# The mish MLP's first product by Strassen's seven block products

## The chip, the cores and the metric

One core of a Trainium2 chip. The metric is the device time of one execution in microseconds, the median of several runs; the profile is that of one execution.

## The reference

Three parts follow one another on 2304 tokens (4 batches of 576): a landmark attention, a gated product, and the mish MLP that the change is in. Weights are given in float64, everything is computed as float32.

```python
x = landmark_attention(q, k, v)            # [2304, 512]
y = ((x @ w1) * (x @ w2) @ w3) @ w_out     # the gated product, [2304, 512]
h = y @ w_in                               # [2304, 2048]
g = h * np.tanh(np.log1p(np.exp(np.minimum(h, 20.0))))   # mish
out = g @ w_out2                           # [2304, 512]
```

## The kernel before, in words

Float32 products are made from float32r matmuls: each operand is split into a high part (a copy, on ACT) and a low part (a difference, on DVE or POOL), and `mm3` (L194 to L197) issues three matmuls, high x high, high x low and low x high. A weight block of 128 x 512 float64 is loaded into a raw buffer as pairs of 32-bit words and decoded to float32 by four steps: `top_bits` (`da`, L207 on ACT or L209 on DVE), `sign` (`dm`, L213, DVE), `rescale` (`ds`, L216, ACT) and `join` (`db`, L220, DVE).

Up to the end of the gated product the order of the work is written out by hand. `step` names a piece of work, `ORDER` (L27) is a long string of these names, and `issue` (L284) emits them one after another; within an engine the instructions run in that order. The steps that the change touches: `m`, `xa`, `xb`, `xc`, `xm` make the gate's halves `h`; `sh u k` and `sl u k` (L913) split `h` for half-batch `u` (288 tokens, eight of them) into one of two buffers; `y u m` (L920) multiplies it by the folded weights, 4 x 24 matmuls of 288 columns for a half-batch, and `ye` evicts the result to `Y`. The last `y` steps, 3 0 to 7 3, run with nothing but splits beside them on TensorE's side: I call them the y stage. `ld x`, `da x`, `dm x`, `ds x`, `db x`, `hi x`, `lo x` bring in and split 32 blocks of the mish weights (`w_in` and `w_out` in turns of four); 26 of them are decoded and 20 split inside `ORDER`, and `yh`, `yl` split the first tile of `Y`.

Then comes the mish stage, emitted by the loop at L1140. Tokens go in tiles of 512 (four and one of 256), `d_ff` in 16 chunks of 128; one pair of tile and chunk is a tick. `p2` (L1117) issues for tick n:

```python
z_mm(n)       # 4 mm3: 12 matmuls into one of banks 0 to 3
o_mm(n - 2)   # one mm3 for each 128 tokens into banks 4 to 7
tick(n)       # ACT: mish twice (L1113, L1114); DVE: their difference (L1115)
```

Beside the first tile's ticks it splits the last 12 weight blocks and decodes the last 6 (loads on SP's queue, as everywhere); at the end of a tile it splits the next tile's `Y` and evicts the output. All split weights then stay in SBUF, in buffers of earlier stages (`wpart`, L949). `swap` (L902) closes the attention's pool and opens the buffers `hs`.

Of the kernel before, what the change touches and what calls it, by code (L numbers as in the profile page):

```python
# [154 lines left out]
def kernel(  # L155
# [883 lines left out]
    for k in range(4):  # L1039
        add_ys(k)  # L1040
# [141 lines left out]
```

## Time and profile before

| | us |
|---|---|
| median of 3 runs | 767.44 |
| lowest and highest | 767.3, 768.48 |
| span of the profiled execution | 765.2 |

The page gives the profiled execution's span, from its first instruction to its last, and no other time for it. In the profile PE is TensorE's matmuls, PEld its weight loads, DVE, ACT and POOL the vector, scalar and GpSimd engines, SP the engine that issues the loads. Durations of matmuls overlap, so the distance between starts says what one costs. "L1113" is a line of the kernel; an operand such as `ps<-hs,W` names the tile written and the tiles read, without buffer numbers, and late tiles have the names `ys`, `wx`, `gx` and the like.

### The profile page before, as it was taken

How to read it: one execution, taken by the hardware profiler on the slowest of the kernel's cores; microseconds unless marked ns; L12 is line 12 of the kernel's file. 1: busy time of each engine (PE TensorE's matmuls, PEld its weight loads, DVE VectorE, ACT ScalarE, POOL GpSimd, SP SyncE). 2: the span in 40 equal slices, each digit the busy share in tenths (PEclk: the TensorE clock that was granted, in tenths of full speed). 3: DMA queues.
4: the chain of work that ended last, by engine and by line, in shares of the span. 5: the costliest groups of instructions: out<-in, count | busy, mean ns of one | idle time of the engine just before them, and what ended most of it. 6: DMA issues, size and time to landing. Idle time of an engine off the chain costs nothing.

```text
span 765.2 us, 12842 instructions
## 1 busy us (share of the span) xinstructions
...
## 2 busy tenths in 40 slices
...
PEclk9999999999999999999999999999999999999999
...
GB/s 329 372 284 69 153 132 250 152 81 142 57 165 139 84 111 52 196 128 122 56 110 0 1 1 55 1 1 0 56 0 1 1 0 56 1 0 1 56 1 28
DMA packets 37243, 65.90 MB, mean 86 GB/s; under 512 B 2624, under 2 KB 19392, under 8 KB 37184
## 3 DMA queue, kind: packets, MB, share of 16 engines
q1 hardware_dynamic: 37040, 64.96, 25.0%
...
## 4 chain that ended last, share of the span: by engine, by line
PE 89%; DMA 6%; DVE 2%; ACT 1%; SPq 0%; issue 0%; ACTq 0%
PE ps L195 27%; PE ps L197 26%; PE ps L196 26%; PE ps L360 4%; DMA raw<-in_w3T_dram 3%; DMA raw<-in_wo_dram 2%; PE ps L851 2%; PE ps L650 1%; PE ps L454 1%; DMA raw<-in_w_dram 1%; DVE raw L213 1%; PE ps L532 1%; PE ps L591 1%; PE ps L510 0%; PE ps L570 0%; ACT raw L207 0%
## 5 line engine op out<-in xcount | busy, mean ns | idle before, releaser
L1113 ACT ACTIVATE emx<-ps 128x512 f32<-128x512 f32 (+1 forms) x80 | 44.3, 554 | 131.5 <-PE ps L197 131.5
L1115 DVE TENSOR_TENSOR gx<-emx,gx 128x512 fp32r<-128x512 f32 (+1 forms) x40 | 25.6, 639 | 155.1 <-ACT gx L1114 155.1
L195 PE MATMUL ps<-hs,W 128*128 128x288 f32 (+2 forms) x304 | 92.9, 306 | 0.0
L196 PE MATMUL ps<-hs,W 128*128 128x288 f32 (+2 forms) x304 | 92.3, 304 | 0.0
L197 PE MATMUL ps<-hs,W 128*128 128x288 f32 (+2 forms) x304 | 92.2, 303 | 0.0
L1115 DVE TENSOR_TENSOR hs<-emx,hs 128x512 fp32r<-128x512 f32 (+1 forms) x40 | 25.5, 639 | 136.6 <-ACT hs L1114 136.6
L213 DVE TENSOR_SCALAR raw<-raw 128x512 uint16<-128x512 uint16 x84 | 67.2, 840 | 29.2 <-ACT raw L207 28.7
L195 PE MATMUL ps<-AT,M 128*128 128x288 f32 x256 | 79.1, 309 | 1.7 <-ACT a L224 1.4
L196 PE MATMUL ps<-AT,M 128*128 128x288 f32 x256 | 75.5, 295 | 0.0
L197 PE MATMUL ps<-AT,M 128*128 128x288 f32 x256 | 75.5, 295 | 0.0
L360 PE MATMUL ps<-wo,raw 128*128 128x512 f32 x128 | 63.2, 617 | 7.2 <-DVE raw L220 5.4
L207 ACT ACTIVATE raw<-raw 128x512 int32<-128x512 uint16 x64 | 43.2, 679 | 50.4 <-DMA raw<-in_w3T_dram 14.6
L216 ACT ACTIVATE raw<-raw 128x512 f32<-128x512 f32 x84 | 55.5, 675 | 19.5 <-DVE raw L213 19.4
L195 PEld LDWEIGHTS ps<-hs,W 128*128 128x128 f32 x304 | 57.0, 188 | 3.0 <-issue 0.4
L196 PEld LDWEIGHTS ps<-hs,W 128*128 128x128 f32 x304 | 57.4, 189 | 1.4
L197 PEld LDWEIGHTS ps<-hs,W 128*128 128x128 f32 x304 | 57.4, 189 | 1.3
L195 PEld LDWEIGHTS ps<-AT,M 128*128 128x128 f32 x256 | 48.0, 188 | 11.8 <-issue 3.7
L196 PEld LDWEIGHTS ps<-AT,M 128*128 128x128 f32 x256 | 48.1, 188 | 0.0
L197 PEld LDWEIGHTS ps<-AT,M 128*128 128x128 f32 x256 | 48.1, 188 | 0.0
L1114 ACT ACTIVATE gx<-ps 128x512 fp32r<-128x512 f32 (+1 forms) x40 | 22.2, 556 | 61.2 <-PE ps L196 61.2
L360 PEld LDWEIGHTS ps<-wo,raw 128*128 128x128 f32 x128 | 22.6, 196 | 28.8 <-issue 15.1
L1114 ACT ACTIVATE hs<-ps 128x512 fp32r<-128x512 f32 (+1 forms) x40 | 22.2, 556 | 54.7 <-PE ps L196 54.7
...
## 6 DMA issues: line engine op xcount, KB each, us to landing
...
raw<-in_wo_dram SPq DMA_DIRECT2D x22, 512.0 KB, 5.3
raw<-in_w3T_dram SPq DMA_DIRECT2D x16, 512.0 KB, 5.3
raw<-in_wi_dram SPq DMA_DIRECT2D x14, 512.0 KB, 4.0
...
```

Of the source, the lines that this page charges most:

```text
L195: T.matmul(out=o, lhsT=lh, rhs=rh, start=first, stop=False)
L196: T.matmul(out=o, lhsT=lh, rhs=rl, start=False, stop=False)
L197: T.matmul(out=o, lhsT=ll, rhs=rh, start=False, stop=last)
L207: S.activation(w[..., 0], q[..., 1], ACTF.Copy, scale=2.0 ** -13, bias=2.0 ** -14 - 0.5)
L213: V.tensor_scalar(q[..., 1], q[..., 3], 0x8000, None, op0=ALU.bitwise_and)
L216: S.activation(f32(w[..., 1]), f32(w[..., 1]), ACTF.Copy, scale=2.0 ** -112)
L360: T.matmul(out=got(f"acc{i}"), lhsT=f32(got(f"w3{n}")[:, o:o + 128, 0]), rhs=WO0[j // 4][:, j % 4], start=j == 0, stop=j == 7)
L454: T.matmul(out=sc[0:w, i, p * 64:p * 64 + 64], lhsT=st["q"][:, p, t0:t0 + w], rhs=bdk[:, p, :], start=True, stop=True)
L851: T.matmul(out=got(f"p{c}{key}")[32 * i:32 * i + 32, 0:256], lhsT=LT[r, b, 2 * c + par, :], rhs=w12(f"w{bp}{s}{c}")[r, par * 256:par * 256 ...
L1113: S.activation(x, zt[n], ACTF.Mish)
L1114: S.activation(gb(n, 0), zt.pop(n), ACTF.Mish)
L1115: V.tensor_tensor(gb(n, 1), x, f32(gb(n, 0)), op=ALU.subtract)
```

## The change

With `Y` and `w_in` cut into blocks (the contraction of 512 in halves; the tokens in halves; 256 of the 2048 features in halves), the four blocks of z come from seven products of block sums in place of eight products. Token tiles become 768, in halves of 384 (`QT`), three of them; a quarter `q` is 256 features, eight of them; a group `g` is one tile and one quarter, 24 in all. In a group:

- `z_mm(g, p, x, first)` is product P0 to P6: 2 `mm3`, 6 matmuls of 384 columns, into bank 0 or 1, cleared before or added to what is there (P2 is added to P0, P3 and P5 to P1, P6 to P4).
- The rest of the recombination is on DVE: `q_`, `r_` and the blocks `c_of(1)` (two halves of 384) and `c_of(0)`, sums of a bank and an earlier sum; ACT copies P0 out to `s_`. Mish is applied to a bank (384), to `c_of(1)` (768) and to `c_of(0)` (384), twice each as before.
- `o_part(g - 1, i)` issues the output product of the group before in four parts of 9 matmuls of 512, into banks 2 to 7. Group 0 has none.
- `more(i)` emits the work of `WITH[g]` (only in the first tile, groups 0 to 7; six lists to a group, divided by `|`).

The weights of a quarter are summed on POOL (`zs0` to `zs3`), each of the seven sums is split by ACT (`zh`) and DVE (`zl`), 256 columns each, and the quarter is stored in DRAM by `zd` (1.8 MB). A block of the output weights is split by `wh` (ACT) and `wl` (POOL) and stored by `ws` (0.5 MB). This happens for quarters 0 and 1 and blocks 0 and 1 inside `ORDER`, for the others in the first tile's groups, with 20 of the 32 decodes. From group 6 on the weights of a group two ahead are loaded from DRAM (`after_z`, and the loop at the end of a group) into slots that the group just read. Seven operands of a tile's `Y` are formed by `yt` (POOL), `yh` (ACT) and `yl` (DVE): inside `ORDER` for the first tile, in `after_z` of groups 7 and 15 for the others. All transfers are on SP's queue, apart from one at the very end.

In `ORDER` the steps `ld x` to `lo x`, and the old `yh` and `yl`, go; in their places stand `ld n` to `db n` of 12 blocks, two `wh`, `wl` and `ws`, the sums and splits of quarters 0 and 1 and the operands of the first tile. The other steps keep their order.

```diff
-EARLY, RAW6 = 20, 6
...
+WITH = (
+    "zs0 2,zs1 2,zs2 2,wh 2,wl 2,da 16|zh0 2,zl0 2,dm 16,ld 18,ws 2|zh1 2,zl1 2,ds 16,wh 3,wl 3,ld 19,ws 3,da 17|zh2 2,zl2 2,db 16,dm 17|zh3 2,zl3 2,zs3 2,ds 17,db 17,da 18,dm 18|zh4 2,zl4 2,zh5 2,zl5 2,zh6 2,zl6 2,zd 2",
+    "zs0 3,zs1 3,zs2 3,ds 18,db 18,ld 12,ld 13|zh0 3,zl0 3,da 19,dm 19|zh1 3,zl1 3,ds 19,db 19,ld 14,ld 15|zh2 3,zl2 3,da 12,dm 12|zh3 3,zl3 3,zs3 3,ds 12,db 12|zh4 3,zl4 3,zh5 3,zl5 3,zh6 3,zl6 3,zd 3,da 13,dm 13,zs0 4,zs1 4,zs2 4",
+    "ds 13,db 13,wh 4,wl 4|zh0 4,zl0 4,da 14,dm 14,ld 24,ws 4|zh1 4,zl1 4,ds 14,db 14,wh 5,wl 5|zh2 4,zl2 4,da 15,dm 15,ld 25,ws 5|zh3 4,zl3 4,zs3 4,ds 15,db 15,da 24,dm 24|zh4 4,zl4 4,zh5 4,zl5 4,zh6 4,zl6 4,zd 4",
+    "zs0 5,zs1 5,zs2 5,ds 24,db 24,wh 6,wl 6,ld 20|zh0 5,zl0 5,da 25,dm 25,ld 26,ws 6|zh1 5,zl1 5,ds 25,db 25,wh 7,wl 7,ld 21|zh2 5,zl2 5,da 26,dm 26,ld 27,ws 7|zh3 5,zl3 5,zs3 5,ds 26,db 26,ld 22,da 27,dm 27|zh4 5,zl4 5,zh5 5,zl5 5,zh6 5,zl6 5,zd 5,ds 27,db 27,ld 23",
+    "zs0 6,zs1 6,zs2 6,da 20,dm 20|zh0 6,zl0 6,ds 20,db 20,wh 8,wl 8|zh1 6,zl1 6,da 21,dm 21,ld 28,ws 8|zh2 6,zl2 6,ds 21,db 21,wh 9,wl 9|zh3 6,zl3 6,zs3 6,da 22,dm 22,ld 29,ws 9|zh4 6,zl4 6,zh5 6,zl5 6,zh6 6,zl6 6,zd 6,ds 22,db 22",
+    "zs0 7,zs1 7,zs2 7,wh 10,wl 10,da 23,dm 23|zh0 7,zl0 7,ds 23,db 23,ld 30,ws 10|zh1 7,zl1 7,da 28,dm 28|zh2 7,zl2 7,ds 28,db 28|zh3 7,zl3 7,zs3 7,wh 11,wl 11|zh4 7,zl4 7,zh5 7,zl5 7,zh6 7,zl6 7,zd 7,ld 31,ws 11",
+    "wh 12,wl 12,da 29,dm 29|ds 29,db 29,ws 12|da 30,dm 30|wh 13,wl 13,ds 30,db 30|da 31,dm 31,ws 13|ds 31,db 31",
+    "wh 14,wl 14||wh 15,wl 15,ws 14||ws 15|",
+MADE = (0, 1, 2, 3, 8, 9, 10, 11, 4, 5, 6, 7, 16, 17, 18, 19, 12, 13, 14, 15, 24, 25, 26, 27, 20, 21, 22, 23, 28, 29, 30, 31)
...
-    TT = 512
+    QT, TT = S_LEN * B // 6, S_LEN * B // 3
...
-    RAW2 = [kept(f"M{i}", [128, 512, 2], I32, f"raw{i}") for i in range(3)]
-    M = {}
+    RAW2 = kept("M", [128, 3, 512, 2], I32, "raw2")
+    M = []
...
-        HS.extend(pw.tile([128, 8 * 2 * HALF], F32R, name=f"hs{i}") for i in range(2))
-        HS.append(pw.tile([128, 4, 1024], F32R, name="wx"))
-        HS.append(pw.tile([128, 2, TT], F32R, name="gx"))
-        HS.append(pw.tile([128, TT], F32, name="emx"))
+        LATE["pw"] = pw
+        HS.extend(pw.tile([128, 8 * 2 * HALF], F32R, tag=f"hs{i}", name=f"hs{i}") for i in range(2))
+        HS.append(pw.tile([128, 7 * 512], F32R, name="zw0"))
+        HS.append(pw.tile([128, 4, 512], F32, name="wf0"))
...
+    def y_op(p, hl):
+        n, i = {0: (("W0", 0), ("W0", 1)), 2: (("W1", 0), ("W1", 1)), 4: (("H1", 0), ("H1", 1)),
+                3: (("H1", 2), ("H2", 0)), 1: (("H2", 1), ("H2", 2)), 5: (("H3", 0), ("H3", 1)),
+                6: (("M", 0), ("H3", 2))}[p][hl]
+        x = at_m() if n == "M" else late(n, 2048 if n[0] == "W" else 2304, f"y{n}")
+        return x[:, i * 768:(i + 1) * 768].rearrange("p (c s) -> p c s", c=2)
...
+    def wo_slot(u):
+        i = u % 7
+        if i == 0:
+            return at_m()[:, 768:1792]
+        if i == 1:
+            return hs_a()[:, 3584:4608]
+        if i < 4:
+            return late("Y0", 2048, "wy")[:, (i - 2) * 1024:(i - 1) * 1024]
+        return at_m()[:, 1792:2816] if i == 4 else w3_flat(i - 5)[:, 3072:4096]
+
+    def zw_slot(g, p):
+        return (hs_a() if g % 2 else HS[2])[:, p * 512:(p + 1) * 512]
...
+        ops = [(f"ld {n}", "SP", lambda e: x_load(n)), (f"da {n}", "ACT", lambda e: top_bits(e, r())),
+               (f"dm {n}", "DVE", lambda e: sign(r())), (f"ds {n}", "ACT", lambda e: rescale(r()))]
+        if k == 0:
+            return ops + [(f"db {n}", "DVE", lambda e: join(r(), wf(j)[:, i]))]
+        return ops + [
+            (f"db {n}", "DVE", lambda e: join(r())),
+            (f"wh {f}", "ACT", lambda e: copy(e, wo_slot(f)[:, 0:512], f32(r()[..., 0]))),
+            (f"wl {f}", "POOL", lambda e: less(e, wo_slot(f)[:, 512:1024], f32(r()[..., 0]), wo_slot(f)[:, 0:512])),
+            (f"ws {f}", "SP", lambda e: nc.sync.dma_start(out=wod[f], in_=f32(wo_slot(f))))]
...
+        a11, a12, a21, a22 = (0, 0), (0, 1), (1, 0), (1, 1)
+        return [(f"zs0 {q}", "POOL", f(0, a21, a22, ALU.add)),
+                (f"zs1 {q}", "POOL", f(1, 0, a11, ALU.subtract)),
+                (f"zs2 {q}", "POOL", f(a21, a11, a21, ALU.subtract)),
+                (f"zs3 {q}", "POOL", f(1, a12, 1, ALU.subtract))]
...
+    def zp_ops(q, p):
+        return [(f"zh{p} {q}", "ACT", lambda e: copy(e, zw(q, p, 0), z_src(q, p))),
+                (f"zl{p} {q}", "DVE", lambda e: less(e, zw(q, p, 1), z_src(q, p), zw(q, p, 0)))]
+
+    def z_store(q):
+        def f(e):
+            x = (hs_a() if q % 2 else HS[2])[:, 0:3584]
+            nc.sync.dma_start(out=zd[q], in_=f32(x))
+        return (f"zd {q}", "SP", f)
...
+        return [(f"yt4 {t}", "POOL", sub_(y_cuts(t, 0, 1), t_(0), b_(0, 1), b_(0, 0))),
+                (f"yt1 {t}", "POOL", sub_(y_cuts(t, 1), t_(1), b_(1, 1), t_(0))),
+                (f"yt3 {t}", "POOL", sub_(y_cuts(t, 1), b_(0, 1), b_(1, 1), b_(0, 1))),
+                (f"yt5 {t}", "POOL", sub_(y_cuts(t, 0), t_(1), b_(1, 0), t_(1)))]
...
-    def z_mm(n):
-        t, f = divmod(n, NFC)
-        c = slice((f % 4) * 128, (f % 4 + 1) * 128)
-        p = zt[n] = bank[n % 4][:, 0:tiles[t][1]]
-        for k in range(4):
-            u = 8 * (f // 4) + k
...
-    def tick(n):
-        x = E[:, 0:tiles[n // NFC][1]]
-        S.activation(x, zt[n], ACTF.Mish)
-        S.activation(gb(n, 0), zt.pop(n), ACTF.Mish)
-        V.tensor_tensor(gb(n, 1), x, f32(gb(n, 0)), op=ALU.subtract)
...
+    z_bank = bank[0:2]
+    o_bank = bank[2:8]
+    ZT = late("A", 3 * QT, "zt", F32)
+    s_, q_, r_ = (ZT[:, i * QT:(i + 1) * QT] for i in range(3))
...
+    def z_mm(g, p, x, first):
+        for c in range(2):
+            mm3(z_bank[x][:, 0:QT], zw(g, p, 0)[:, c], zw(g, p, 1)[:, c], y_op(p, 0)[:, c], y_op(p, 1)[:, c],
+                first and c == 0, c == 1 and p in (2, 5, 6), True)
+
...
+    def o_part(g, part):
+        if g < 0:
+            return
+        t, q = divmod(g, NQ)
+        if q < NQ - 1:
+            e, i0 = ((0, 0), (1, 0), (1, 3), (0, 3))[part]
+            for i in range(i0, i0 + 3):
+                o_mm(g, e, i)
+            return
+        for i in ((0, 1), (2,), (3, 4), (5,))[part]:
+            for e in range(2):
+                o_mm(g, e, i)
+            o_out(t, i)
+
+    def mish(src_, e, o):
+        S.activation(e, src_, ACTF.Mish)
+        S.activation(o, src_, ACTF.Mish)
...
+    NG = 3 * NQ
+    for g in range(NG):
+        t, q = divmod(g, NQ)
+        todo = WITH[g].split("|") if g < NQ else [""] * 6
+        if q == 5 and t < 2:
+            run(ysum_ops(t + 1)[:3])
+
+        def more(i):
+            for name in filter(None, todo[i].split(",")):
+                name, _, at_e = name.partition("@")
+                e, fn = ops.pop(name)
+                fn(at_e or e)
+
+        def after_z(p):
+            if g + 2 < NG and g + 2 >= NQ:
+                nc.sync.dma_start(out=f32(zw_slot(g + 2, p)), in_=zd[(g + 2) % NQ][:, p * 512:(p + 1) * 512])
+            if q == NQ - 1 and t < 2:
+                run(yp_ops(t + 1, p))
+                if p == 1:
+                    run(ysum_ops(t + 1)[3:])
+
+        z_mm(g, 0, 0, True)
+        S.activation(s_, z_bank[0][:, 0:QT], ACTF.Copy)
+        after_z(0)
+        z_mm(g, 1, 1, True)
+        V.tensor_tensor(q_, z_bank[1][:, 0:QT], s_, op=ALU.add)
+        after_z(1)
+        more(0)
+        o_part(g - 1, 0)
+        more(1)
+        z_mm(g, 2, 0, False)
+        mish(z_bank[0][:, 0:QT], e_of(0), g_of(g, 0, 0)[:, 0:QT])
+        after_z(2)
+        z_mm(g, 3, 1, False)
+        V.tensor_tensor(r_, z_bank[1][:, 0:QT], s_, op=ALU.add)
+        less("DVE", g_of(g, 0, 1)[:, 0:QT], e_of(0), g_of(g, 0, 0)[:, 0:QT])
+        after_z(3)
+        more(2)
+        o_part(g - 1, 1)
+        more(3)
+        z_mm(g, 4, 0, True)
+        after_z(4)
+        z_mm(g, 5, 1, False)
+        after_z(5)
+        V.tensor_tensor(c_of(1)[:, QT:2 * QT], z_bank[0][:, 0:QT], r_, op=ALU.add)
+        V.tensor_tensor(c_of(1)[:, 0:QT], z_bank[1][:, 0:QT], s_, op=ALU.add)
+        mish(c_of(1), e_of(2), g_of(g, 1, 0))
+        more(4)
+        o_part(g - 1, 2)
+        z_mm(g, 6, 0, False)
+        after_z(6)
+        V.tensor_tensor(c_of(0), z_bank[0][:, 0:QT], q_, op=ALU.add)
+        less("DVE", g_of(g, 1, 1), e_of(2), g_of(g, 1, 0))
+        mish(c_of(0), e_of(1), g_of(g, 0, 0)[:, QT:TT])
+        less("DVE", g_of(g, 0, 1)[:, QT:TT], e_of(1), g_of(g, 0, 0)[:, QT:TT])
+        o_part(g - 1, 3)
+        if g:
+            for u in (2 * g - 2 + 7, 2 * g - 1 + 7):
+                if 16 <= u < 2 * NG:
+                    nc.sync.dma_start(out=f32(wo_slot(u)), in_=wod[u % 16])
+        more(5)
```

## Rows read from the trace of the kernel before

**Rows 1.** The page's first line.

```profile
span 765.2 us, 12842 instructions
```

**Rows 2.** Busy time by engine in one stretch; then clock, DMA share, GB/s.

```profile
640.00:680.00 40.00, 40.00 (x178) 33.12 (x177) 6.21 (x10) 9.45 (x17) 0.00 (x0) 1.00 0.00 0
```

**Rows 3.** Timeline of TensorE: start, duration, line, tile, shape.

```profile
366.84 0.30 PE L196 MATMUL ps<-hs,W 128*128 128x288 f32 x1
...
367.89 0.39 PE L195 MATMUL ps<-hs,wx 128*128 128x512 f32 x1
...
600.00 0.39 PE L196 MATMUL ps<-W,hs 128*128 128x512 f32 x1
...
611.79 0.39 PE L197 MATMUL ps<-W,hs 128*128 128x512 f32 x1
...
752.81 0.28 PE L195 MATMUL ps<-hs,W 128*128 128x256 f32 x1
...
754.13 0.28 PE L197 MATMUL ps<-hs,W 128*128 128x256 f32 x1
...
760.95 0.39 PE L197 MATMUL ps<-hs 128*128 128x512 f32 x1
```

**Rows 4.** Groups of ACT by form: count, busy us, mean ns.

```profile
L216 ACT ACTIVATE raw<-raw 128x512 f32<-128x512 f32 x84 | 55.5, 675 | 19.5 <-DVE raw L213 19.4
...
L1114 ACT ACTIVATE gx<-ps 128x512 fp32r<-128x512 f32 x32 | 19.1, 598 | 55.0 <-PE ps L196 55.0
...
L224 ACT ACTIVATE hs<-y 128x512 fp32r<-128x512 f32 x4 | 2.4, 624 | 0.0
...
L224 ACT ACTIVATE hs<-y 128x256 fp32r<-128x256 f32 x4 | 1.6, 409 | 0.0
```

**Rows 5.** Timeline of ACT at the start of the mish stage.

```profile
368.52 1.28 ACT L1113 ACT_TABLE_LOAD   x1
370.81 0.60 ACT L1113 ACTIVATE emx<-ps 128x512 f32<-128x512 f32 x1 [1.01 <-PE ps L197]
371.31 0.59 ACT L1114 ACTIVATE gx<-ps 128x512 fp32r<-128x512 f32 x1
```

**Rows 6.** Groups of DVE by form.

```profile
L889 DVE TENSOR_TENSOR h<-a,ps 128x288 f32<-128x288 f32 x64 | 28.5, 453 | 17.2 <-PE ps L197 13.7 <-ACT M L224 2.0 <-ACT a L224 1.0
...
L229 DVE TENSOR_TENSOR hs<-y,hs 128x512 fp32r<-128x512 f32 x4 | 2.7, 702 | 0.2 <-ACT hs L224 0.2
...
L229 DVE TENSOR_TENSOR hs<-y,hs 128x256 fp32r<-128x256 f32 x4 | 1.7, 419 | 0.0
```

**Rows 7.** Groups of POOL by form.

```profile
L229 POOL TENSOR_TENSOR hs<-raw,hs 128x512 fp32r<-128x512 f32 x2 | 2.6, 1302 | 7.8 <-ACT hs L224 7.8
```

**Rows 8.** The page's DMA queues and DMA issues.

```profile
q1 hardware_dynamic: 37040, 64.96, 25.0%
...
raw<-in_wi_dram SPq DMA_DIRECT2D x14, 512.0 KB, 4.0
```

**Rows 9.** Timelines of DVE and POOL, around 225 us and 380 us.

```profile
225.17 0.88 DVE L229 TENSOR_TENSOR hs<-h,hs 128x288 fp32r<-128x288 f32 x1
...
229.53 0.45 DVE L229 TENSOR_TENSOR hs<-h,hs 128x288 fp32r<-128x288 f32 x1
...
224.93 0.80 POOL L229 TENSOR_TENSOR hs<-h,hs 128x288 fp32r<-128x288 f32 x1
...
356.70 0.77 DVE L213 TENSOR_SCALAR raw<-raw 128x512 uint16<-128x512 uint16 x1 [0.72 <-ACT raw L207]
...
380.77 1.58 DVE L213 TENSOR_SCALAR raw<-raw 128x512 uint16<-128x512 uint16 x1
...
379.98 1.76 POOL L229 TENSOR_TENSOR W<-raw,W 128x512 fp32r<-128x512 f32 x1 [3.40 <-ACT W L224]
```

**Rows 10.** TensorE's waits (total, times, longest us); the page's clock in 40 slices.

```profile
PE ps L360 <- DVE raw L220: 5.4, 3, 3.2
...
PEclk9999999999999999999999999999999999999999
```

More of the change, by code (lines that the diff above doesn't have):

```diff
@@ new lines, in cut, with y_at @@
+    def cut(t, h):
+        a, out_ = t * TT + h * QT, []
+        end = a + QT
+        while a < end:
+            b, s = divmod(a, S_LEN)
+            n = min(end - a, S_LEN - s)
+            out_.append((a - t * TT - h * QT, n, b, s))
+            a += n
+        return out_
+    def y_at(t, k, h, lo, n):
+        for o, m, b, s in cut(t, h):
+            if o <= lo and lo + n <= o + m:
+                return Y[b][:, 2 * k:2 * k + 2, s + lo - o:s + lo - o + n]
+        raise AssertionError
@@ new lines, in y_parts, with yp_ops, hi, lo @@
+    def y_parts(t, p):
+        if p in (1, 4, 5):
+            return [(slice(0, QT), lambda: y_sum(0 if p == 4 else 1))]
+        k, h = {0: (0, 0), 2: (1, 0), 3: (0, 1), 6: (1, 1)}[p]
+        return [(slice(a, z), lambda a=a, z=z: y_at(t, k, h, a, z - a)) for a, z in y_cuts(t, h)]
+    def yp_ops(t, p):
+        def hi(e):
+            for s, x in y_parts(t, p):
+                copy(e, y_op(p, 0)[:, :, s], x())
+        def lo(e):
+            for s, x in y_parts(t, p):
+                less(e, y_op(p, 1)[:, :, s], x(), y_op(p, 0)[:, :, s])
+        return [(f"yh{p} {t}", "ACT", hi), (f"yl{p} {t}", "DVE", lo)]
```

295 lines of the change are left out of this document (167 added, 128 removed), and 233 rows, old and new, of the table ORDER.

## The prediction

> **What bounds the kernel now.** I read the page first, then stretches of the last stage, then single instructions. The execution in the profile spans 765.2 us [rows 1]; the median of the runs is 767.44, so I take 2.24 us as lying around the span and leave it unchanged. In the mish stage TensorE is busy in all of a 40 us stretch while ACT and DVE are busy about a quarter and a sixth of it, and the clock is full [rows 2]. So the stage lasts as long as its matmuls, and their price is the step from one start to the next, not the printed duration, which overlaps: for 512 columns 0.2267 us (600.00 to 611.79 is 52 steps), for 256 0.120 (752.81 to 754.13, 11), for 288 0.131 (366.84 to 367.89, 8) [rows 3]. From 288 to 512 that is 0.427 ns a column, so 384 columns should step by 0.131 + 96 x 0.000427 = **0.172 us**; 0.170 and 0.175 are the ends that the rounding of the rows allows. The stage runs from 367.89 to 760.95 plus one step, 761.18: 393.3 us [rows 3]. Counted from the code: z takes 64 ticks x 12 matmuls of 512 and 16 x 12 of 256, 768 x 0.2267 + 192 x 0.120 = 197.1 us; the output product 864 of 512, 195.9. The sum, 393.0, leaves no gap.
>
> **What the change takes off TensorE.** z becomes 3 tiles x 8 quarters = 24 groups of 7 products of 6 matmuls of 384 columns: 1008 x 0.172 = 173.4 us. The output product keeps its 864. TensorE's own work falls by 197.1 - 173.4 = **23.7 us** (20.7 to 25.7 for the ends of the step). A group is now 7.2 us of z and 8.2 of output, 15.4. The y stage just before keeps TensorE's steps and loses work beside them: from `y 3 0` on 17 decodes and 11 splits go, 3 decodes, 14 splits of 256 and 7 of 768 come (20 of the 32 decodes now fall into the first tile of the mish stage, where 6 did). Its five half-batches of 12.6 us (96 x 0.131) cover that, since the splits that one waits for stand a half-batch early: nothing, and 1 us if the cover is thin.
>
> **What it adds elsewhere.** Before, z needed no adds and had four banks. Now it has two, and the same bank is read, then added to, then cleared, so each product waits for an ACT or DVE read. Prices: an ACT pair of Mish on 384 columns 0.49 us each (0.60 for 512 less 128 columns at the slope of the copies), the second starting before the first ends as at 512 (0.50 after it, of 0.60) [rows 4, 5]; a copy from SBUF 0.41 for 256 and 0.62 for 512, so 0.84 for 768; a decode's ACT step 0.68 [rows 4]. On DVE an add of 384 is 0.56, a split of 256 0.42, a split of 768 0.98, a decode step 0.77 [rows 6, 9]. ACT starts about 0.2 us after the last matmul of a product (12 steps after 367.89 is 370.61, Mish at 370.81) [rows 3, 5]. On POOL a split of 512 is 1.30 [rows 7]; a sum of 256 I take as 0.8, a little over half of that. A loaded block of 512 KB lands in 4.0 us; queue 1 moved 64.96 MB in a quarter of the span, so 340 GB/s when it moves [rows 8].
>
> In **tiles 1 and 2** a group's load is some 4 us on ACT and 5 on DVE, of 15.4. The tightest loop is P5 to the next P0: DVE takes the two halves, 0.75 us after P5; Mish on 768 twice, to 2.4; P6 and its add to 3.9; TensorE comes back to that bank at 2.04 + 1.03 + 2.04 = 5.1. No wait. Reloading weights is 2.9 MB a group, 8.5 us at 340 GB/s, ordered a group and more ahead: nothing, and the whole of it shows only if a load lands 15 us late.
>
> **Group 0** has no output product to fill the waits. Count from P0's start (a product is 1.03 us). ACT: copy of P0 to 1.7, then `wh 2`, `da 16`, `zh0 2`, which stand ahead of Mish, to 3.2, the table load of 1.28 [rows 5] to 4.4, Mish twice to 5.3. P4 clears that bank; TensorE was free at 4.1: 1.25 us. P4, P5 to 7.4. P6 adds to P4's bank after DVE has read it; ahead on DVE are `zl1 2`, `zl2 2` (for which ACT first does `zh1`, `ds 16`, `wh 3`, `da 17`, `zh2`, to 7.65), `db 16`, `dm 17`; the read ends at 9.75: 2.4 us. P6 to 10.8. The next P0 needs DVE's last add, and ahead of that are `zl3 2`, `db 17` and `dm 18`, behind ACT's Mish on 768 (10.3 to 11.9), `zh3 2`, `ds 17`, `da 18`; it ends at 14.5: 3.7 us. Together **7.3**. With none of those extras in the way the same chain gives 1.0, and with each decode step on DVE stretched as below, 10.
>
> **Groups 1 to 6.** 9 output matmuls (2.04 us) now stand between the products, and by the same count a group without a late load waits 0.1 to 0.5: the chain Mish on 768, `zh3`, `ds`, `da`, `dm`, last add is 5.0 us against TensorE's 5.1. Two groups are worse, for what is queued behind what on SP: the store of a quarter's weight sums (`zd`, 1.8 MB, 5.4 us) waits for the last split and stands ahead of loads. In group 1 `ld 12` goes behind `zd 2`, lands about 9 us into the group, and ACT reaches `da 12` 2 us before; the delay passes through `dm 12` and Mish on 768: 2.0 us. In group 3 `ld 26` waits for `wl 6` on POOL and goes behind `zd 4` and `ld 20`: 2.3 us. No row shows such a store; if it held up nothing, both would cost 0.3. The other four take 1.2 together.
>
> POOL works 6.5 us in each of these groups (4 sums, 2 splits), and beside POOL DVE slows: a split of 288 took 0.88 against 0.45 alone, a decode step 1.58 against 0.77, and POOL's own 1.30 became 1.76 [rows 7, 9]. I charge 0.3 us in five groups, 1.5; the ends are 0 and 3 a group (rival below). The Trainium skill (SBUF — State Buffer, "SBUF: two separate sides") says that this is a lock: a GpSimd instruction and a DVE one with two SBUF inputs hold the shared ports in turn, whole instructions at a time. The rows agree with that; taken for every DVE split it gives the second rival's time and not mine.
>
> **Groups 7 and 15** make the next tile's seven operands, a copy and a split of 768 behind each product, and those for P5 and P6 stand ahead of the adds: after P5 a copy to 1.0, a split to 2.0, the read of P4's bank at 2.5, 0.5 us past TensorE's return; then P6's copy (behind Mish) and split, the last add at 6.8 where TensorE is back at 5.6: 1.2. 1.7 each, **3.4** (0 to 5). The tail is the same 4 us: last matmul, a half-bank copy, a store.
>
> Sum: 767.44 - 23.7 + 7.3 + 2.0 + 2.3 + 1.2 + 1.5 + 3.4 = **761.4 us**.
>
> **Rivals.** *The covers hold*: engines run ahead more than I count, so that group 0 costs 5 and the transitions 3.4, the rest 1: 767.44 - 23.7 + 9.4 = 753.1. For it: my chains in groups 1 to 6 miss by tenths only. Against: group 0 has no output product.
>
> *DVE behind POOL sets the first tile's pace* (slower). If every split and decode step of a group meets a POOL instruction: nine splits x 0.43, 2.5 joins x 0.33 (taken a little under the split's), 2.5 sign steps x 0.81, 6.7 us on DVE's 11.6 is 18.3 against 15.4: 3 us in each of six groups instead of the 7.0 in all: 761.4 - 7.0 + 18 = 772.4. It decides from 2.2 us a group, (6.0 + 7.0) / 6, where the gain is gone. For it: the rows named. Against: POOL works under half the time.
>
> *The clock falls* in group 0's waits. The longest wait of TensorE in this trace is 3.2 us and every slice of the page shows full clock [rows 10], so none is charged; mine is 3.7. If the two products and nine output matmuls that follow (4.1 us) ran at the lower level, 1.2 for 2.4 GHz, they would take twice that: 765.5. The Trainium skill (TensorE: Matmul & The Clock Gate, "Part 1: The HAM clock gate") has the clock halve after an idle stretch; no run here shows it.
>
> *It doesn't do what it says*: the shorter matmul keeps more of the longer one's step than the line says. A step of 0.190 makes z 191.5 and the time 779.5. The 256 and 288 rows [rows 3] speak against it.
>
> **How the numbers follow.** Forecast 0.48 (757 to 766), covers hold 0.24, DVE behind POOL 0.18 (of it 0.07 no change), clock 0.07, no shorter step 0.03. About 0.2% (1.5 us) is what a measurement of this kernel can tell from no change. Faster: 0.46 + 0.24 + 0.06 = 0.76; same: 0.02 + 0.07 + 0.01 (the forecast's upper end, part of DVE's, the clock's rest) = 0.10; slower: 0.11 of DVE's and 0.03 = 0.14. The range 752 to 770 takes the forecast and the clock whole, most of the covers' case and the nearer half of DVE's, and leaves out about 0.08 below and 0.12 above. The likeliest case's own is 757 to 766.
>
> **What would show it.** In the profile after: 384-column starts 0.172 apart, z busy from group to group in tiles 1 and 2, 15.4 us each; three waits of TensorE in group 0, the last on DVE's add, some 7 us in all; waits of 2 us in groups 1 and 3 traced to ACT's `da` behind a load; 1.7 at both tile changes. Wrong if the steps are longer, if tiles 1 and 2 wait for DMA, or if the first tile's groups all take 18 us (then DVE and POOL are to be looked at).

## The result and the profile after

The changed kernel takes **776.71 us**, the median of 4 runs (774.72 to 777.52), against 767.96 for the kernel before (767.30 to 768.56): ratio 1.0109, 95% interval 1.0086 to 1.0132. It is slower, where 761.4 was forecast and the range ended at 770. The profiled execution took 775.96 and spans 774.2 us; against [rows 1] that is 9.0 more. The mish stage now runs from 368.78 to 770.08, 401.3 us instead of 393.3, and starts 0.9 later: both together are the whole difference. The forecast gave that stage 387.3, so it came out 14.0 too long.

Of the page: the first line, TensorE's busy time, its slices with the granted clock, and the queue that carries the loads (compare [rows 1, 8, 10]).

```profile
span 774.2 us, 13579 instructions
...
PE 739.4 (96%) x5236; PEld 623.0 (80%) x5236; DVE 454.2 (59%) x870; ACT 346.0 (45%) x753; POOL 158.6 (20%) x176
...
PE   6998999999999999999699889989999999999997
...
PEclk8999999999999999999899999999999999999999
...
q1 hardware_dynamic: 61232, 134.17, 51.4%
```

TensorE is still busy nearly everywhere, with a hole in slice 20 (group 0) and shallow ones in slices 23, 24 and 27, all in the first tile. Its waits, in the view that lists them (engine, tile and line waited for; us in total, times, longest), are new ones on DVE's last adds, L1339 and L1332:

```profile
PE ps L198 <- DVE hsb L1339: 9.4, 5, 3.0
PE ps L198 <- DVE hsb L1332: 6.7, 4, 2.9
...
PE ps L198 <- ACT W L1273: 1.0, 1, 1.0
```

Cutting the timeline of TensorE at the first matmul of each P0 gives the length of every group. A settled group, one in the middle of tile 1 or 2 that waits for nothing, takes 15.71 us, not 15.4. The first row of the table is the changed kernel; the other rows belong to the experiments below, and the last column is the mish stage as a whole. The last tile's final group, with the tail, is 23.6 us in all of them.

| kernel | g0 | g1 | g2 | g3 | g4 | g5 | g6 | g7 | g15 | settled | stage |
|---|---|---|---|---|---|---|---|---|---|---|---|
| the change | 15.3 | 17.2 | 17.2 | 20.3 | 18.8 | 17.4 | 15.7 | 18.2 | 17.4 | 15.71 | 401.3 |
| e2 stores behind loads | 15.4 | 18.4 | 16.6 | 21.8 | 19.4 | 17.4 | 15.7 | 18.2 | 17.4 | 15.71 | 404.1 |
| e6 store in seven parts | 15.4 | 18.5 | 16.6 | 19.6 | 19.0 | 17.4 | 15.7 | 18.2 | 17.4 | 15.71 | 401.5 |
| e9 fewer bytes in g3 | 15.4 | 18.6 | 16.6 | 16.4 | 18.9 | 17.3 | 15.7 | 18.2 | 17.4 | 15.71 | 398.3 |
| e3 token sums later | 15.4 | 18.2 | 16.6 | 21.5 | 15.8 | 15.7 | 16.9 | 18.3 | 17.4 | 15.71 | 399.5 |
| e7 longer runs of a width | 15.3 | 17.9 | 16.0 | 20.1 | 18.9 | 17.3 | 15.7 | 18.2 | 17.4 | 15.57 | 399.7 |
| e4 side work later | 8.3 | 16.7 | 15.8 | 15.7 | 19.6 | 24.1 | 16.2 | 19.9 | 17.4 | 15.71 | 397.5 |
| e8 and new tile change | 8.3 | 16.7 | 15.8 | 15.9 | 16.8 | 21.0 | 17.2 | 17.9 | 15.7 | 15.71 | 389.1 |
| e10 version | 8.3 | 16.7 | 15.8 | 15.9 | 18.9 | 16.8 | 20.3 | 21.6 | 15.7 | 15.57 | 392.3 |
| e12 e8 and longer runs | 8.3 | 16.7 | 15.8 | 15.9 | 16.5 | 21.0 | 17.4 | 17.8 | 15.7 | 15.57 | 387.5 |
| e11 version, spread | 8.3 | 16.7 | 15.8 | 15.9 | 17.7 | 17.4 | 17.3 | 16.3 | 15.7 | 15.57 | 383.2 |

One caution for all of them: the code ahead of the mish stage is the same, yet that stage started anywhere from 367.8 to 371.5 us. So a change of 2 us is read from the stage and the groups, and the medians are named beside it. In brackets behind a median stand its ratio to the kernel before and the 95% interval of that.

**The steps.** TensorE's timeline in a settled group (start, duration): the last output matmul, P0, the first and last of P1, the first of the output part behind it.

```profile
655.92 0.39 PE L200 MATMUL ps<-ym,W 128*128 128x512 f32 x1
656.15 0.33 PE L198 MATMUL ps<-yW,hs 128*128 128x384 f32 x1
...
657.22 0.33 PE L198 MATMUL ps<-yH,hs 128*128 128x384 f32 x1
...
658.09 0.33 PE L200 MATMUL ps<-yH,hs 128*128 128x384 f32 x1
658.26 0.39 PE L198 MATMUL ps<-W 128*128 128x512 f32 x1
...
659.88 0.40 PE L199 MATMUL ps<-W 128*128 128x512 f32 x1
```

P0's six steps take 1.07 us, 0.178 each; P1's take 1.04, 0.1733. Seven output steps take 1.62, 0.231 each, where [rows 3] had 0.2267. P2, P4 and P6 are like P0, P3 and P5 like P1. Over 640 to 740 us the means are 0.1757 and 0.231. I call the dearer steps lifted.

**The clock.** Stretches of the trace: busy us (count) of PE, PEld, DVE, ACT, POOL, then granted clock, DMA share, GB/s.

```profile
375.00:380.00 5.00, 2.12 (x12) 1.80 (x12) 3.46 (x6) 1.55 (x5) 2.17 (x2) 1.00 0.82 241
380.00:385.00 5.00, 1.97 (x8) 1.46 (x7) 3.00 (x5) 3.79 (x8) 0.00 (x0) 0.53 0.34 136
385.00:390.00 5.00, 5.00 (x22) 4.61 (x21) 4.19 (x8) 2.86 (x8) 2.28 (x3) 0.79 0.44 184
430.00:440.00 10.00, 7.36 (x29) 5.95 (x28) 5.01 (x9) 5.11 (x10) 0.00 (x0) 0.83 0.76 294
...
460.00:470.00 10.00, 10.00 (x47) 9.03 (x47) 8.65 (x14) 5.22 (x12) 4.90 (x5) 0.89 0.74 273
```

Behind waits of 2.8 to 3.4 us the granted clock falls to about its lower level, 1.2 GHz, three times: a 384-column step is then 0.31 to 0.32 us, an output step 0.43. The clock in [rows 10] has no such slice.

**Group 0.** TensorE's timeline, the three matmuls that wait:

```profile
374.20 0.44 PE L198 MATMUL ps<-yH,zw 128*128 128x384 f32 x1 [1.04 <-ACT W L1273]
...
379.43 0.44 PE L198 MATMUL ps<-ym,zw 128*128 128x384 f32 x1 [2.88 <-DVE hsb L1332]
...
384.10 0.69 PE L198 MATMUL ps<-yW,hs 128*128 128x384 f32 x1 [3.04 <-DVE hsb L1339]
```

Measured from start to start less a step they are 1.2, 3.05 and 3.4, 7.6 us.

**Groups 3 and 4.** SP's and ACT's timelines in group 3: the store `zd 4`, the load `ld 26` behind it, and ACT's `da 26` that waits for the load:

```profile
421.56 0.33 SPq L1063 DMA_DIRECT2D zd<-zw  x1
...
425.04 0.33 SPq L1010 DMA_DIRECT2D raw<-in_wi_dram  x1
...
432.05 0.67 ACT L210 ACTIVATE raw<-raw 128x512 int32<-128x512 uint16 x1 [4.85 <-DMA raw<-in_wi_dram]
```

And the end of group 4, POOL's token sums for the next tile and DVE's work beside them:

```profile
452.76 1.85 POOL L1037 TENSOR_TENSOR sums<-y,y 128x768 f32<-128x768 f32 x1
454.69 1.86 POOL L1037 TENSOR_TENSOR sums<-y,sums 128x768 f32<-128x768 f32 x1
456.52 2.17 POOL L1037 TENSOR_TENSOR y<-y 128x768 f32<-128x768 f32 x1
...
452.95 1.95 DVE L232 TENSOR_TENSOR zw<-wf,zw 128x256 fp32r<-128x256 f32 x1 [2.01 <-ACT zw L227]
454.82 2.33 DVE L216 TENSOR_SCALAR raw<-raw 128x512 uint16<-128x512 uint16 x1
456.95 0.57 DVE L1339 TENSOR_TENSOR hsb<-ps,zt 128x384 f32<-128x384 f32 x1
```

A split that is 0.42 alone [rows 6] takes 1.95 and a decode step of 0.77 [rows 9] takes 2.33; the add that TensorE waits for stands behind them.

### The profile page after: what moved, and what is told of

The parts are those of the page before. It is cut to its first block, busy times and chain, and to the rows that moved or that the text cites. A ratio compares the mean times of both kernels' runs of the same rounds, so it can differ in the third digit from the quotient of the medians.

```text
span 774.2 us, 13579 instructions
## 1 busy us (share of the span) xinstructions
PE 739.4 (96%) x5236; PEld 623.0 (80%) x5236; DVE 454.2 (59%) x870; ACT 346.0 (45%) x753; POOL 158.6 (20%) x176
## 4 chain that ended last, share of the span: by engine, by line
PE 79%; DMA 7%; DVE 6%; ACT 4%; issue 2%; POOL 0%; SPq 0%; ACTq 0%; POOLq 0%; DVEq 0%
PE ps L198 23%; PE ps L200 23%; PE ps L199 23%; PE ps L363 4%; DMA raw<-in_w3T_dram 3%; DMA raw<-in_wo_dram 3%; PE ps L854 2%; DVE raw L216 2%; DMA raw<-in_w_dram 1%; PE ps L653 1%; DMA raw<-in_wi_dram 1%; ACT W L1273 1%; PE ps L457 1%; DVE yH L232 1%; ACT raw L219 1%
## 5 line engine op out<-in xcount | busy, mean ns | idle before, releaser
L198 PE MATMUL ps<-hs,W 128*128 128x288 f32 (+1 forms) x298 | 92.7, 311 | 0.0
L199 PE MATMUL ps<-hs,W 128*128 128x288 f32 (+1 forms) x298 | 92.1, 309 | 0.0
L200 PE MATMUL ps<-hs,W 128*128 128x288 f32 (+1 forms) x298 | 92.1, 309 | 0.0
L1272 ACT ACTIVATE hsb<-hsb 128x768 f32<-128x768 f32 (+1 forms) x48 | 32.9, 686 | 124.3 <-DVE hsb L1333 87.6
L216 DVE TENSOR_SCALAR raw<-raw 128x512 uint16<-128x512 uint16 x88 | 72.8, 862 | 24.7 <-ACT raw L210 24.4
L219 ACT ACTIVATE raw<-raw 128x512 f32<-128x512 f32 x88 | 58.7, 676 | 25.6 <-DVE raw L216 25.6
L210 ACT ACTIVATE raw<-raw 128x512 int32<-128x512 uint16 x72 | 48.3, 673 | 43.3 <-DMA raw<-in_w3T_dram 14.9
L198 PEld LDWEIGHTS ps<-hs,W 128*128 128x128 f32 x298 | 56.2, 188 | 3.0 <-issue 0.8
L200 PEld LDWEIGHTS ps<-hs,W 128*128 128x128 f32 x298 | 56.3, 189 | 1.7
L199 PEld LDWEIGHTS ps<-hs,W 128*128 128x128 f32 x298 | 56.5, 190 | 1.5
L232 DVE TENSOR_TENSOR W<-hsb,W 128x384 fp32r<-128x384 f32 (+1 forms) x72 | 53.4, 744 | 5.2 <-ACT W L1273 4.8
L363 PEld LDWEIGHTS ps<-wo,raw 128*128 128x128 f32 x128 | 23.6, 204 | 30.7 <-issue 17.2
L227 ACT ACTIVATE a<-ps 128x288 f32<-128x288 f32 x64 | 26.2, 411 | 39.3 <-PE ps L200 36.9
L1322 DVE TENSOR_TENSOR zt<-ps,zt 128x384 f32<-128x384 f32 x24 | 13.4, 559 | 51.5 <-PE ps L200 51.5
L892 DVE TENSOR_TENSOR h<-a,ps 128x288 f32<-128x288 f32 x64 | 28.4, 452 | 21.4 <-PE ps L200 18.0
```

The lines of the kernel that those rows point to most:

```text
L198: T.matmul(out=o, lhsT=lh, rhs=rh, start=first, stop=False, skip_group_check=partial)
L199: T.matmul(out=o, lhsT=lh, rhs=rl, start=False, stop=False, skip_group_check=partial)
L200: T.matmul(out=o, lhsT=ll, rhs=rh, start=False, stop=last, skip_group_check=partial)
L210: S.activation(w[..., 0], q[..., 1], ACTF.Copy, scale=2.0 ** -13, bias=2.0 ** -14 - 0.5)
L216: V.tensor_scalar(q[..., 1], q[..., 3], 0x8000, None, op0=ALU.bitwise_and)
L219: S.activation(f32(w[..., 1]), f32(w[..., 1]), ACTF.Copy, scale=2.0 ** -112)
```

## The experiments

**What lifts the steps.** Behind the last store the kernel's own matmuls run again in ten blocks, each opened by one matmul of 128 columns.

```diff
+    block(od=False); block(); block(swap_=1); block(sp=1); block(sp=0)
+    block(mp=1); block(mp=0); block(wide=True); block(on=384); block()
```

> Behind the last store of the output, the changed kernel's own matmuls are issued again in ten blocks with nothing on the other engines: z products alone; the kernel's order (z, z, 9 output matmuls and so on); the same with the two z banks exchanged; with the weights of P1, then of P0, for every product; with the tokens of P1, then of P0, for every product; with z widened to 512; with the output part narrowed to 384; the kernel's order once more. In the kernel 384-column steps are 0.1777 us in P0, P2, P4, P6 and 0.1733 in P1, P3, P5, and 512-column steps 0.231 where the kernel before had 0.2267. Theory 'mixed widths': z alone and both single-width blocks give 0.173 and 0.227, every mixed block 0.1755 and 0.231, whatever banks and operands. Rival 'bank 0': with the banks exchanged P1, P3, P5 are the slow ones. Rival 'place of an operand in SBUF': the block with P1's weights (or tokens) for all has every product at 0.1733, the one with P0's has every product at 0.1777. Rival 'the other engines': all blocks at 0.173 and 0.227.

Mean steps in ns (the first product of a block stands behind the 128-column matmul):

| block | P1, P3, P5 | P2, P4, P6 | output |
|---|---|---|---|
| z alone | 173.3 | 173.3 | none |
| kernel's order (both times) | 173.3 | 177.5 to 177.7 | 231.1 to 231.2 |
| banks exchanged | 173.3 | 177.5 to 177.7 | 231.1 to 231.2 |
| P1's or P0's weights, P1's or P0's tokens | 173.3 | 177.5 to 177.7 | 231.1 to 231.2 |
| z of 512 | 226.7 | 226.7 | 226.7 |
| output of 384 | 173.3 | 173.3 | 173.3 |

The probe's timeline: P0, P1 and the output part in the kernel's order, with nothing on another engine.

```profile
792.40 0.39 PE L198 MATMUL ps<-yW,hs 128*128 128x384 f32 x1
792.63 0.33 PE L199 MATMUL ps<-yW,hs 128*128 128x384 f32 x1
...
793.50 0.33 PE L198 MATMUL ps<-yH,hs 128*128 128x384 f32 x1
...
794.54 0.39 PE L198 MATMUL ps<-ym,W 128*128 128x512 f32 x1
...
796.62 0.33 PE L198 MATMUL ps<-yW,hs 128*128 128x384 f32 x1
```

P1's six steps are 1.04 us, the nine output steps 2.08, 0.231 each. Only the mixture of widths matters; banks, operands and the other engines' work are out. A single width steps by 0.1733 or 0.2267 throughout. How far a lift reaches, the next kernel shows.

**Longer runs of one width.** In the groups of tiles 1 and 2 that neither begin nor end a tile (12; the expectation's 13 is a miscount) the order of the matmuls changes as below, in short, with o9 for nine output matmuls; one of DVE's adds also goes ahead of P5:

```diff
-P0 P1 o9 P2 P3 o9 P4 P5 o9 P6 o9
+P0 P1 P2 P3 o18 P4 P5 P6 o18
```

> In 13 settled groups of tiles 1 and 2 the order P0 P1 o9 P2 P3 o9 P4 P5 o9 P6 o9 becomes P0 to P3, o18, P4 to P6, o18: two changes each way between the widths in place of four, the same matmuls. Theory 'the lift of 4.4 ns a step lasts for some matmuls behind a change of width' (at most 12 of 512, 6 of 384): 36 + 24 lifted steps a group become at most 24 + 12, the group falls from 15.70 to 15.59 us or less, the whole by 1.4 us or more, to 775. Rival 'the lift lasts as long as widths are mixed at all': groups stay at 15.70. Rival 'the bank is not read in time where P2 follows P1 at once': groups rise by 0.2 or more, with waits at P2 and P4.

Nine of these groups fall to 15.57 us and the stage from 401.3 to 399.7; the median, 776.74 (1.0117, 1.0100 to 1.0134), shows nothing, as its stage started at 371.54. By place in a run, the first nine steps of 512 have a mean of 0.231 and the other nine 0.2267; the first six of 384 have 0.177 and nearly all later ones 0.1733; three groups keep a wait of 0.2 to 0.3 more. So a change of width costs nine steps of 512 or six of 384 some 4.4 ns each, exactly as many as the kernel's runs of output matmuls had, which is why its whole output part was lifted. 30 lifted steps fewer a group are 0.13 us.

**The clock alone.** Extra matmuls fill group 0's waits:

```diff
+        if g == 0: warm(5)    # ahead of P4
+        if g == 0: warm(15)   # ahead of P6
+        if g == 1: warm(16)   # ahead of P0
```

> The changed kernel with 36 extra matmuls of 384 columns into a bank that is free then, 5 before P4 and 15 before P6 of group 0, 16 before P0 of group 1: they fill most of TensorE's three waits (1.2, 3.05 and 3.4 us) and change nothing else. Theory 'the clock falls in the waits and the steps after them are slow for it': the granted clock stays full from 375 to 390 us, the 384-column steps of P6, P0 and P1 are 0.175 instead of 0.31, and groups 0 and 1 together take 1.5 to 2 us less: about 775. Rival 'the steps are slow for what the other engines do then': the steps stay above 0.25 and the time is the changed kernel's 776.7 or up to 1 us more, since the extra matmuls end a little after the wait.

The same stretches as above:

```profile
375.00:380.00 5.00, 4.67 (x27) 4.35 (x26) 3.61 (x6) 1.68 (x4) 2.20 (x2) 1.00 0.67 216
380.00:385.00 5.00, 4.41 (x25) 4.09 (x25) 2.91 (x6) 3.61 (x7) 0.00 (x0) 1.00 0.39 152
385.00:390.00 5.00, 5.00 (x28) 4.61 (x27) 4.86 (x9) 3.08 (x9) 2.74 (x3) 1.00 0.37 152
```

The clock stays full, so the waits were its cause. The first output matmul comes 1.26 us earlier (17.61 behind the stage's start instead of 18.87). But the 72 output matmuls behind it take 34.41 us instead of 33.00, with new waits on DVE's adds; the stage is 401.7 and the median 775.54 (1.0110, 1.0097 to 1.0124). What holds group 1 up now is a load: `da 12` waits for `ld 12`, which stands behind the store `zd 2`, and the adds stand behind `da 12`. ACT's row of it, first in the changed kernel, then here:

```profile
395.15 0.66 ACT L210 ACTIVATE raw<-raw 128x512 int32<-128x512 uint16 x1 [2.11 <-DMA raw<-in_wo_dram]
...
395.55 0.67 ACT L210 ACTIVATE raw<-raw 128x512 int32<-128x512 uint16 x1 [3.53 <-DMA raw<-in_wo_dram]
```

In the changed kernel TensorE has no wait inside group 1: its 1.5 us over 15.7 are slow steps, and they hide the late load. So the slow clock cost nothing there while that load was late. In group 5, which has no wait either and was 17.4 with a clock of 0.89, it did cost: 1.7 us.

**The loads behind a store.** First the order on SP, with three stores behind the loads:

```diff
-...,zd 4|zs0 5,zs1 5,zs2 5,ds 24,db 24,wh 6,wl 6,ld 20|...,ld 26,ws 6|
+...|wh 6,wl 6,ld 26,zs0 5,zs1 5,zs2 5,ds 24,db 24,ld 20,zd 4|...,ws 6|
```

> Only SP's order changes, and `wl 6` goes ahead of three sums on POOL: the stores of the weight sums of quarters 2, 3 and 4 stand behind the loads `ld 13`, `ld 24` and `ld 26` instead of ahead of them. Theory 'loads behind the store': group 3 falls from 20.3 us by its wait of 2.8 and most of the slowed steps after it (1.5), group 1 from 17.2 by up to 1.4; in all 4 to 5.5 us below the changed kernel, 771 to 773. Rival 'DVE and POOL set those groups': under 1 us, group 3 stays above 19.

777.61 (1.0133, 1.0111 to 1.0155): a miss, and group 3 got longer. In group 1 no load is late any more, yet it takes 18.4 us, with 16 slow steps behind group 0's waits (2.4 us) where the changed kernel's profile has 8 (1.1 us); e6 and e9 show the same. In group 3, ACT's timeline (two `da`, the second for `ld 27`, issued at 428.16):

```profile
427.36 0.69 ACT L210 ACTIVATE raw<-raw 128x512 int32<-128x512 uint16 x1 [0.61 <-DMA raw<-in_wi_dram]
...
438.31 0.65 ACT L210 ACTIVATE raw<-raw 128x512 int32<-128x512 uint16 x1 [5.38 <-DMA raw<-in_wi_dram]
```

`ld 26` was in time; `ld 27`, now the one behind the store, took 10.2 us from issue. The lateness moved on to the next load. Then the store in pieces:

```diff
+            if q > 1:
+                nc.sync.dma_start(out=zd[q][:, p * 512:(p + 1) * 512], in_=f32(zw_slot(q, p)))
```

> The store of a quarter's weight sums (1.8 MB in one piece behind its last split) becomes seven of 256 KB, each issued behind its own split, so that at a group's end only the last three are outstanding. Theory 'a load that stands behind the store is late': in group 3 `ld 26` lands in time, the wait of 2.8 us goes and with it the slowed steps (1.5), group 1 loses up to 1.4 less: 771 to 773. Rival 'the bytes of group 3 are too many, wherever the store stands': another load is late instead, as when the store stood behind `ld 26`, group 3 stays above 19 us and the time within 1.5 of 776.7.

774.98 (1.0099, 1.0083 to 1.0114), group 3 at 19.6: `ld 26` took 5.9 us and `ld 27` 7.0, both late, and two waits of 1.7 and 2.0 us stand where there was one of 2.8. That is the rival's case, with the time 0.2 us below its bound. So fewer bytes ahead of these two loads:

```diff
-...,wh 6,wl 6,ld 20|...,ld 26,ws 6|...,wh 7,wl 7,ld 21|...,ld 27,ws 7|
+wh 6,wl 6,ld 26,zs0 5,...|...|...,wh 7,wl 7,ld 27|...,ld 20,ld 21|
+zs0 6,zs1 6,zs2 6,da 20,dm 20,ws 6,ws 7|
```

> As with the store in seven parts, and besides, `wl 6` and `ld 26` go ahead of the sums of quarter 5, `ld 20` and `ld 21` behind `ld 27`, and the stores `ws 6` and `ws 7` into group 4: what stands ahead of `ld 26` and `ld 27` falls by some 2 MB. With one store the loads `ld 26` and `ld 27` took 7 and up to 10 us from issue, in seven parts 5.9 and 6.9. Theory 'the bytes asked for in group 3 are too many, wherever the store stands': both land within 5 us, group 3 with its two waits falls from 19.6 us to 16.5 or less, nothing else moves: 3 us below the store in seven parts, 771 to 773. Rival 'the chain of decodes, sums and adds on ACT, DVE and POOL sets group 3 as well': it stays above 18.5 and no load ends a wait of ACT.

Group 3 falls to 16.4 and nothing else moves; 771.13 (1.0049, 1.0033 to 1.0065). Of the same two `da` the first waits 0.25 us for its load, issued at 424.36, and the second not at all:

```profile
428.82 0.69 ACT L210 ACTIVATE raw<-raw 128x512 int32<-128x512 uint16 x1 [0.25 <-DMA raw<-in_wi_dram]
...
434.66 0.66 ACT L210 ACTIVATE raw<-raw 128x512 int32<-128x512 uint16 x1
```

Both loads were also issued earlier in the group than in seven parts (by 2.4 and 1.0 us); what of the 3.2 us is due to that and what to the bytes isn't told apart.

**The token sums.**

```diff
-        if q == 5 and t < 2:
+        if q == 5 and t == 1:
             run(ysum_ops(t + 1)[:3])
...
         more(1)
+        if q == 6 and t == 0:
+            run(ysum_ops(t + 1)[:3])
```

> The three token sums on POOL for the second tile (128x768, 1.85 us each) are issued in the middle of group 6 instead of at the head of group 5, from where POOL ran them in group 4. Theory 'these sums hold up DVE': group 4 falls from 18.8 to 15.8, the slowed steps in group 5 (1.7 us) go too, group 6 rises by under 1: 4 us in all, about 772.5. Rival 'the collision only moves': group 4 falls, group 6 rises by 2 to 3: 774 to 776. Rival 'group 4 waits for its own work': group 4 stays over 18.

772.97 (1.0076, 1.0060 to 1.0091). Groups 4 and 5 fall to 15.8 and 15.7, by 4.7 us together; group 6 rises by 1.2. DVE's two instructions, at 453.38 and 453.95 in this trace, are 0.43 and 0.76 again. Group 3 was 21.5 here, with the same wait of 2.8 and a longer spell of the low clock: how much such a spell costs differs from run to run.

**Group 0's side work.** All of `WITH` four slots later:

```diff
+for _n, _s in enumerate("|".join(WITH).split("|")):
+    _m = _n + (5 if _n == 0 else 4 if _n < 30 else 3 if _n < 36 else 2 if _n < 41 else 1 if _n == 41 else 0)
+    SLOTS[_m] = ",".join(x for x in (SLOTS[_m], _s) if x)
...
-        todo = WITH[g].split("|") if g < NQ else [""] * 6
+        todo = LATER[g].split("|") if g < NQ else [""] * 6
```

> All side work of the first tile (decodes, weight sums, splits, stores) is issued four of the six slots of a group later, the last ones less; nothing of it stands ahead of a Mish or an add of group 0. Theory 'group 0 loses by what stands ahead on ACT and DVE': group 0 falls from 15.3 us to 9 to 10, with one wait of 0.5 to 1 before P6, the clock stays full in groups 0 and 1 (1.3 us more), groups 1 to 6 keep their waits: 769 to 771. Rival 'the load only moves': groups 1 to 7 take it as waits, and the time stays within 2 us of the changed kernel's 776.7.

771.03 (1.0046, 1.0030 to 1.0062). Group 0 is 8.3 us, with a single wait:

```profile
376.15 0.44 PE L204 MATMUL ps<-yW,hs 128*128 128x384 f32 x1 [0.65 <-DVE hsb L1345]
```

Groups 0 to 3 together gain 13.4 us with a full clock; groups 4, 5, 6 and 7 give back 9.6: in group 4 ACT waits 3.0 us for a load, in group 5 output blocks come late and meet the token sums, and the clock falls in both. Theory and rival are each half right.

**Putting it together.** To the side work later come the token sums on DVE, `ld 26` and `ld 27` early, and the next tile's operands behind the adds:

```diff
+        mish(c_of(1), e_of(2), g_of(g, 1, 0))
+        next_y(4)
...
+        next_y(5)
+        next_y(6)
```

> Side work of the first tile four slots later; `ld 26` and `ld 27` ahead of `ld 20` and `ld 21`; the three token sums for the second tile on DVE in the middle of group 6; in groups 7 and 15 the next tile's operands of P4, P5 and P6 behind the adds and the Mish instead of ahead of them. Theory 'each excess of a group over 15.7 us has its own cause, named so far': group 0 8.3, group 1 16.7, groups 2 to 6 15.7 to 16.5 each with full clock, groups 7 and 15 16.0 or less: 755 to 758, below the kernel before. Rival 'ACT and DVE are too full in the first tile for any order': groups 2 to 7 keep 6 us or more over 15.7 each in all and the time is above 763.

763.49 (0.9956, 0.9941 to 0.9971): below the kernel before, above what was expected. Group 15 loses its excess whole; groups 4 to 7 keep 10 us over 15.7 each, the rival's case for this order. A new layout of those,

> Built on the kernel with the side work later: in groups 3 to 7 the side work is laid out again so that the blocks 20 and 21, which the output product needs first, are loaded and decoded ahead of 26 and 27, and quarter 6's sums come a group later; P0 to P3, o18, P4 to P6, o18 in the settled groups; in groups 7 and 15 every operand of the next tile stands behind the adds. Theory 'what was left over 15.7 us in groups 4 to 7 (2.2, 4.2, 1.5, 2.2) came from late blocks and from operands ahead of the adds': these four fall to 2 us or less together, the settled groups to 15.58: 8 to 10 us below that kernel, 754 to 756. Rival 'ACT, DVE and the loads are too full there in any order': the four keep 6 us or more, and the time is 759 or above.

gave 765.36 (0.9967, 0.9952 to 0.9981), a miss: group 5 fell from 21.0 to 16.8, but groups 6 and 7 took more work than they had room for (20.3 and 21.6, of which 2.6 are slow steps in group 7). Longer runs added to e8 alone,

> The kernel with the side work later and the new tile change (763.5), with two changes alone: P0 to P3, o18, P4 to P6, o18 in the 13 settled groups, and in groups 7 and 15 the operands of P0 to P3 too behind the adds. Theory 'the parts add': settled groups 15.58 instead of 15.70 (1.6 us), group 7 a wait of 1.4 less: 760.5 to 761.9. Rival: the new order costs waits in the first tile or at the tile change, and the time is 763.5 or above.

gave 762.31 (0.9934, 0.9920 to 0.9949), between theory and rival: the stage fell by the 1.6 us of the steps; the wait at the change of tile only moved to the adds. The last layout spreads quarters 6 and 7 over groups 5 and 6:

```diff
-"zs0 6,zs1 6,zs2 6,da 22,dm 22,ld 29|zh0 6,zl0 6,zh1 6,zl1 6,ds 22,db 22|"
+"ds 27,db 27,zs0 6,zs1 6,zs2 6,ws 8,ld 29|zh0 6,zl0 6,zh1 6,zl1 6,da 22,dm 22,ws 9|"
...
-"wh 11,wl 11,ws 10,ld 31,zs0 7,zs1 7,zs2 7|zh0 7,zl0 7,da 28,dm 28,ws 11|"
+"zs0 7,zs1 7,zs2 7,ds 23,db 23,ws 10|zh0 7,zl0 7,wh 11,wl 11,ld 31,ws 11|"
```

> The version before with groups 4 to 7 laid out once more: quarter 6's sums a group earlier than there, quarter 7's from the end of group 5, the three token sums on DVE one by one, `wl 13` half a group earlier, the stores in seven parts and `ws 6`, `ws 7` later. Theory 'groups 6 and 7 of that version (20.3 and 21.5 us) were overfull by its layout alone': groups 4 to 7 together fall from 77.4 us to 68 or less, the clock stays full, 755 to 757. Rival 'the first tile's side work doesn't fit': they stay above 73, 761 or more.

**756.96 us** (755.09 to 758.28; ratio 0.9862, 0.9844 to 0.9880), the best of all: 1.4% below the kernel before. Groups 4 to 7 are 68.7 us together, just above the 68 of the theory. Several things change in it at once, so the gain isn't shared out among them. From its page, and then from TensorE's waits:

```profile
span 755.2 us, 13662 instructions
...
PEclk8999999999999999999999999999999999999999
```

```profile
PE ps L218 <- DVE hsb L1376: 3.5, 6, 1.3
PE ps L218 <- DVE hsb L1365: 1.9, 2, 1.1
```

The clock is full in every slice of the mish stage, and the two waits on DVE's adds that were 9.4 and 6.7 us are 3.5 and 1.9.

## Why the prediction was wrong

The stage came out 14.0 us over and started 0.9 later than before; the terms below add up to 14.2 for the stage.

- **TensorE's price, 0.172 a step and the output product "keeps its 864" at 0.2267: this is the step that failed first.** 1008 x 0.0037 + some 830 x 0.0044 = 7.4 us of the expected 23.7 were never there. The line between two widths was nearly right (0.1733 in a run of one width, 1.3 of the 7.4); the other 6.1 are the mixture: that a stage of two widths is dearer for both was not asked. The trace before shows it: in its last tile the six output matmuls between the 256-column ones take 1.38 us, 0.230 each, from 754.25 to 755.63 (TensorE's timeline of the kernel before), right behind the last of the 256-column rows in [rows 3]:

```profile
754.25 0.40 PE L195 MATMUL ps<-hs,gx 128*128 128x512 f32 x1
...
755.63 0.28 PE L195 MATMUL ps<-hs,W 128*128 128x256 f32 x1
```

- **Groups 2, 4, 5 and 6 (1.2, and most of the 1.5 for DVE beside POOL): 6.3 instead of 2.7.** The next tile's token sums on POOL were not in the sum. They stand at the head of group 5 in the code and ran in group 4; e3 takes 4.7 us off groups 4 and 5. DVE slowed beside POOL, which the forecast took as a rival for every split, did decide group 4, by three long sums. Group 2's 1.5 is a wait on DVE's last add, with splits of 1.55 and 1.54 us ahead of it beside POOL's of 1.54 and 1.61; no run takes that alone away. The Trainium skill (SBUF — State Buffer, "SBUF: two separate sides") has the shared ports held for a whole instruction; 0.42 becoming 1.95 beside a sum of 1.85 agrees.
- **Group 3 (2.3): 4.6.** The mechanism was right, `da 26` behind `ld 26` behind `zd 4`, a wait of 2.8; the other 1.7 are slow steps behind it, which the sum did not have. But taking the store out of the way lost time (e2) and cutting it gained 0.6 us (e6); fewer bytes ahead of both loads, issued earlier, gained 3.2 more (e9). The forecast priced a place in a queue where it should have added up what the group asks for.
- **Group 0 (7.3): 7.6 in three waits,** on the instructions named, 7.9 with the slower steps. Right; e4 shows that what stood ahead on ACT and DVE made nearly all of it.
- **Group 1 (2.0): 1.5.** The late load is there as forecast, ACT waits 2.1 us for it; but TensorE does not see it, since its own slow steps make the 1.5. That the sizes agree is luck. With a full clock the load shows on TensorE (e5, 1.3 us of waits).
- **Groups 7 and 15 (3.4): 4.2.** Right in kind; e8 shows it for group 15.
- **The clock: uncharged, a rival at 7%.** It fell three times. It cost 1.7 in group 5 and nothing in groups 0 to 2 beside the late `ld 12` (e5); where that load is in time, group 1 is 18.4 to 18.6 with the slow steps (e2, e6, e9) and 16.7 with a full clock and the side work later (e4). In group 3 it isn't told apart from the late loads. The Trainium skill (TensorE: Matmul & The Clock Gate, "Part 1: The HAM clock gate") has the clock halve behind idle time: 0.53 behind waits of 3.05 and 3.4 us agrees, and e5 takes it away by filling them.
- **DVE behind POOL in every group (772.4)** did not happen: with the sums gone groups 4 and 5 stand at 15.8 and 15.7. **No shorter step (0.190)** did not either. Tiles 1 and 2 never wait for DMA, as predicted, at twice the traffic.

So the sign was lost in two halves: 7.4 us for steps of which the trace before gave a sign, and 6.8 in the first tile, above all for the token sums and the clock, which were not in the sum. Either half alone would have left the time at about 768 to 769, inside the range.
